# The opening of a fused attention and feed-forward kernel gets another order of instructions on all five engines

## The chip, the cores and the metric

The kernel runs on one core of a Trainium2 chip. The metric is the time of one execution on the device in microseconds (us). The engines of a core are TensorE (PE in the profile; its weight loads are PEld), VectorE (DVE), ScalarE (ACT), GpSimd (POOL) and SyncE (SP), which issues DMAs. Each engine runs its own list of instructions strictly in the order of the list; an instruction that needs the result of another engine waits for a semaphore, and whatever stands behind it on its engine waits too. So the order of each list matters.

## The reference

For 2048 tokens of width 640, the output is the input plus an attention plus a feed-forward layer, both on the normalised input:

```
xn = layernorm(x)
out = x + A(xn, wq, wk, wv, wo) + B(xn, w1, b1, w2, b2)
# A: 32 heads of 20, one K and one V that all heads share
p = softmax((xn@wq per head) @ (xn@wk).T * 20**-0.5);  A = (p @ (xn@wv)) @ wo
# B: hidden width 1536
B = relu(xn@w1 + b1)**2 @ w2 + b2
```

Data are bfloat16.

## The kernel before, in words

**Tiles.** Attention is cut into 32 blocks: 4 groups of 512 queries by 8 groups of 4 heads. In a block the 2048 keys are 16 tiles of 128 (`kt`). The scores of one head and one key tile are one matmul of 128 x 512 into a PSUM bank. A score step `QKj` makes two of them (two heads), and `ACTj` on ScalarE (line 1328) takes both banks at once, writes exp to two slots of `PT`, and so frees the banks. When all four heads of a key tile are there, `PVb_kt` multiplies them with V into PSUM bank 7, where a block's sum grows; this frees the slots. To spare ScalarE, some key tiles go another way (`DQK`, `D1`, `P1` to `P3`, `AD`, `DPV`): VectorE makes a first approximation of exp by arithmetic on bits (`D1`), three shifted copies are made by integer adds on GpSimd or VectorE (`P1` to `P3`, lines 1571 and 1572), and `DPV` multiplies them with V.

**The opening.** The input comes in rows of 128 tokens (`X`, 16 of them). For each row, VectorE takes statistics (`Sa`, `Sb`, `AG`, lines 806 to 808; for rows 2 and 4 ScalarE does, lines 801 and 802), small steps prepare them (`VE`, `NM`), a power gives the reciprocal deviation (`PW` on GpSimd, line 820; for the first four rows `LN` and `EX` on ScalarE), and `XN` writes the normalised row (line 822, on VectorE or GpSimd). TensorE turns it (`T`, lines 866 and 934), VectorE or ScalarE copies that out of PSUM (`TE`), and TensorE makes K (`K`, `KT`), V (`V`) and queries (`Q`, `QC`) from it, which are copied out in turn (`KTe`, `Ve`, `Qe`, `QCe`). `NKr` and `NKs` make the mean of the first keys, which all `KTe` need. The first scores (`QK0`) need the first K and the queries of the first 512 tokens. The first four rows go through first; the other rows are worked in between the first block's scores. Behind them begin the first pieces of the feed-forward layer (`FFN3_f.dt`; `FFN3_f` reads chunk f // 3 of w1, so `FFN3_3` is the first to read chunk `w11`).

**DMA and library.** SyncE issues the loads. `xb` is a copy of the input in DRAM to which GpSimd's `XA` (line 1153) adds the bias by an accumulating DMA of 2.6 MB. `LIB` loads GpSimd's library with the integer add; every pass on GpSimd stands behind it.

**Fills.** Fills are matmuls that TensorE runs while it would wait, to stay busy. A warm-up fill (line 905) writes the bank of the PV sums and is harmless before the first PV step; it may carry a wait on VectorE, taken over from the step it once stood behind. A zero fill (line 901, in the profile under line 729) adds zeros to an open sum; it is harmless only between a block's first and last PV step.

**What sets the order.** A greedy planner first lists all steps with an engine, a duration and what they depend on. Then `PLAN` reorders each engine's list: its tables are strings of small numbers, and each number takes the entry at that place among those that are left (`unpack`; "0*39" takes the first one 39 times). ScalarE has no table, so its list stays as the planner made it. The string "on" chooses for each pass on which engine it runs, and "held" gives each step of GpSimd a step of VectorE that it waits for, or none. `replay` then gives banks and buffers out, and merges the lists; of those, the instructions are made with the waits that are needed.

```
seq[e] = [old[k] for k in unpack(PLAN[e], len(old))]
```

Of the kernel before, what the change touches and what calls it, by code (L numbers as in the profile page):

```python
# [299 lines left out]
def replay(seq, pool, order_all, upool):  # L300
# [32 lines left out]
    while True:  # L333
# [224 lines left out]
def bass_parallel_sum__grouped_kv_mqa__dense_activation_squared_relu__prompt_kernel(nc, A_x, A_wq, A_wk, A_wv, A_wo, B_x, B_w1, B_b1, B_w2, B_b2, out):  # L558
    es = ExitStack()
    with es:  # L560
# [1146 lines left out]
        while True:  # L1707
# [61 lines left out]
            elif unit[0] is not None:  # L1769
# [3 lines left out]
                o = Op(f"{u.name}.{u.k}", "PE", dur, ch())  # L1773
# [368 lines left out]
        fins = replay(seq, pool, order_all, upool)  # L2142
        MODEL["fins"] = fins
        for es_ in ends_of.values():
            es_.sort(key=lambda o: o.start)
            for o in es_:
                o.ends[0], o.ends[1] = o is es_[0], o is es_[-1]
        open_, kept = set(), []
        for o in order_all:
            if o.sums is not None:  # L2150
                (open_.discard if o.ends[1] else open_.add)(0)
            if o.name == "fill" and o.tail and not open_:
                continue
            kept.append(o)
# [99 lines left out]
```

## Time and profile before

| | us |
|---|---|
| median of 3 runs | 665.14 (664.26 to 666.17) |
| the profiled execution | 664.67 |
| its span, first to last instruction | 662.9 |
| first exponential starts | 12.17 |
| TensorE busy | 655.0 (99%) |
| ScalarE busy | 649.2 (98%) |
| VectorE busy | 627.0 (95%) |
| GpSimd busy | 533.1 (80%) |

A row of the timeline gives the start in us, the length in us, the engine, the line of the kernel, the operation, what it writes and reads, its shape and how many like it are merged in the row; a bracket at the end tells how long the engine stood idle before and what ended that. A row of stages gives from and to, the length, the busy time (and the number of instructions) for each engine asked for, the granted TensorE clock, the busy share of the DMA engines and GB/s. Matmuls overlap, so their lengths say less than the distance from one start to the next. `zeros` are zero fills, `hT_tmp,OR` warm-up fills, `qT,kT` scores, `PT,vx` PV steps, `xnT,wk_c` pieces of K, `ident,big` the turning of normalised rows.

### The profile page before, as it was taken

To read this page: it belongs to the slowest core of one execution; us is meant where nothing else is said; L and a number is where in the kernel's file an instruction comes from. 1 tells how busy PE (TensorE), PEld (TensorE's weight loads), DVE (VectorE), ACT (ScalarE), POOL (GpSimd) and SP (SyncE) were. 2 spreads that over 40 slices of the span, in tenths; PEclk is the share of its full clock that TensorE was granted. 3 is DMA by queue.
4 is the path that set the end of the run, shared out by engine and by line. 5 is a ranking of instruction groups with operands and counts; after the bars stand their busy time and mean duration, and the time that the engine had idled before them with its cause. 6 is when DMAs were issued, how large, how long until landed. Compare 5 with 4: busy or idle time off the path is not lost. (4 is left out here: it accounts for less than half of the span.)

```text
span 662.9 us, 22377 instructions
## 1 busy us (share of the span) xinstructions
PE 655.0 (99%) x9569; PEld 212.6 (32%) x9570; DVE 627.0 (95%) x1125; ACT 649.2 (98%) x719; POOL 533.1 (80%) x528
## 2 busy tenths in 40 slices
PE   8999999999999999999999999999999999999997
PEld 4432222332322223333332222333233322223444
DVE  8979999999999999999999999999999999999997
ACT  7999999999999999999999999999999999999995
POOL 1629899898998889898999988888899989799300
PEclk9999999999999999999999999999999999999999
DMA  8694967788997995786956645798798655858731
GB/s 262 188 238 113 189 126 161 163 183 190 191 192 162 184 182 114 135 177 124 184 103 152 126 92 102 153 180 176 150 176 167 130 123 98 171 104 183 136 113 68
DMA packets 53528, 102.09 MB, mean 154 GB/s; under 512 B 15916, under 2 KB 31164, under 8 KB 53364
## 3 DMA queue, kind: packets, MB, share of 16 engines
q0 software_dynamic: 18544, 68.17, 55.7%
q1 hardware_dynamic: 34308, 32.11, 16.7%
q8 instruction: 75, 1.23, 0.8%
q10 hardware_dynamic: 576, 0.38, 0.2%
q14 instruction: 25, 0.20, 0.1%
HBM read 23.26 MB, written 10.01 MB: 50 GB/s over the span
## 5 line engine op out<-in xcount | busy, mean ns | idle before, releaser
L1328 ACT ACTIVATE PT<-ps 128x1024 bf16<-128x1024 f32 x696 | 640.1, 1125 | 1.8 <-PE ps L729 1.4
L1551 DVE TENSOR_SCALAR tx<-ps 128x512 uint16<-128x512 f32 x656 | 423.7, 682 | 20.8 <-PE ps L729 13.5
L1571 POOL INT64_ADD tx<-tx x369 | 391.2, 1130 | 56.7 <-PE ps L729 16.4
L729 PE MATMUL ps<-qT,kT 20*128 20x512 bf16 x2048 | 263.5, 385 | 0.3
L729 PEld LDWEIGHTS ps<-qT,kT 20*128 20x128 bf16 x2048 | 67.8, 91 | 253.1 <-ACT PT L1328 133.5
L729 PE MATMUL ps<-PT,vx 128*32 128x512 bf16 x1392 | 131.4, 384 | 0.0
L729 PE MATMUL ps<-tx,vxs 128*32 128x512 bf16 x1220 | 113.0, 384 | 0.6 <-DMA tx<-tx 0.5
L1588 POOL DMA_DIRECT2D tx<-tx x103 | 102.4, 994 | 7.7 <-POOL tx L1571 6.9
L729 PE MATMUL ps<-w_sb,big 128*32 128x320 bf16 x1536 | 82.7, 302 | 0.0
L729 PE MATMUL ps<-tx,vx 128*32 128x512 bf16 x864 | 81.3, 384 | 0.8 <-DMA tx<-tx 0.7
L729 PE MATMUL ps<-xnT,w_sb 128*32 128x512 bf16 x960 | 79.0, 383 | 0.0
L1572 DVE TENSOR_SCALAR tx<-tx 128x2048 uint16<-128x2048 uint16 x91 | 63.0, 705 | 0.5 <-DMA tx<-tx 0.3
L729 PEld LDWEIGHTS ps<-PT,vx 128*32 128x32 bf16 x1392 | 34.4, 95 | 39.5 <-issue 35.0
L729 PEld LDWEIGHTS ps<-w_sb,big 128*32 128x32 bf16 x1536 | 34.2, 96 | 30.9 <-issue 20.7
L729 PEld LDWEIGHTS ps<-tx,vxs 128*32 128x32 bf16 x1220 | 28.7, 95 | 36.6 <-issue 27.7
L1054 DVE TENSOR_SCALAR hT_tmp<-ps,b1col 128x512 bf16<-128x512 f32 x48 | 35.7, 743 | 1.5 <-PE ps L729 1.3
L729 PE MATMUL ps<-xnT,wq_sb 128*32 128x512 bf16 (+2 forms) x480 | 35.6, 356 | 0.0
L729 PE MATMUL ps<-wo_c,OC 128*32 128x320 bf16 x576 | 31.8, 301 | 0.0
L2117 POOL INT64_ADD tx<-tx x16 | 30.6, 1913 | 0.5
L729 PEld LDWEIGHTS ps<-tx,vx 128*32 128x32 bf16 x864 | 21.0, 95 | 27.1 <-issue 20.5
L729 PEld LDWEIGHTS ps<-xnT,w_sb 128*32 128x32 bf16 x960 | 19.4, 95 | 25.7 <-issue 17.4
L1416 DVE COPY OR<-ps 128x512 f32<-128x512 f32 x30 | 20.4, 681 | 0.9 <-PE ps L729 0.6
(91 smaller groups left out, 242.3 us busy)
## 6 DMA issues: line engine op xcount, KB each, us to landing
tx<-tx POOLq DMA_DIRECT2D x111, 512.0 KB, 5.8
tx<-tx POOLq DMA_DIRECT2D x7, 1024.0 KB, 9.3
w_sb<-in_B_w_dram SPq DMA_DIRECT2D x8, 480.0 KB, 9.3
big<-OR SPq DMA_DIRECT2D x71, 40.0 KB
xb<-in_A_x_dram SPq DMA_DIRECT2D x1, 2560.0 KB, 12.7
xb<-b2r POOLq DMA_DIRECT2D x1, 2560.0 KB, 19.1
xr<-xb SPq DMA_DIRECT2D x16, 160.0 KB, 3.5
out_dram<-out_sb SPq DMA_DIRECT2D x15, 160.0 KB, 3.3
```

The lines of the kernel that those rows point to most:

```text
L729: return lambda e: e.matmul(out_(), l, val(r), start=val(start), stop=val(stop), tile_position=tp, skip_group_check=loose)
L1054: o = Op(f"RL{qc}_{f}", "DVE", 0.66, [lambda e: e.tensor_scalar(out=hT_tmp[:, k % 2, :], in0=ps[:, at(bk), :], scalar1=b1col[:, f:f + 1], ...
L1328: o = Op(f"ACT{st_['j']}", "ACT", ACB + ACM * n, [lambda e: e.activation(out=PT[:, slots[0].n:slots[0].n + n, :], in_=src(), func=AF.Exp, ...
L1416: tn = op(f"TN{b}", "DVE", 0.60, lambda e: e.tensor_copy(out=OR[:, a, :], in_=ps[:, PVB, :]), [lastpv] + or_users[a], prio=0)
L1551: d1 = op(f"D1_{n}_{i}", "DVE", 0.60, lambda e: e.tensor_scalar(out=L()[:, cs].bitcast(U16), in0=ps[:, ref.n, :], scalar1=XA, scalar2=XB, ...
L1571: fns = dict(POOL=lambda e, T=T, j=j: e.int64_add(out=T().bitcast(I64), in0=L().bitcast(I64), in1=TSTEP * j * 0x0001000100010001), DVE=lam ...
L1572: DVE=lambda e, T=T, j=j: e.tensor_scalar(out=T().bitcast(U16), in0=L().bitcast(U16), scalar1=TSTEP * j, scalar2=None, op0=ALU.add))
L1588: p = op(f"AD{a}_{n}", "POOL", ADDUR, lambda e, src=src, dst=dst: e.dma_start(dst(), src(), accum_op=ALU.add), dp + [ad_last.get(k)], dma= ...
L2117: fn = lambda e, x=x: e.int64_add(out=two(*sorted((x["ref"][2].n, x["ref"][3].n))).bitcast(I64), in0=two(*sorted((x["ref"][0].n, x["ref"][ ...
```

## The change

The tables of `PLAN` get other numbers at their beginning, ScalarE gets a table, and the rule that takes fills out is extended. Reading the tables against the planner's list gives this:

- The same steps remain, fills aside. TensorE's first 264 entries differ (of 3205), the 2941 behind are the same in the same order; ScalarE: the first 42 of 719; VectorE: the first 166 of 1125; GpSimd: the first 39; SyncE: the first 33 of 501.
- Pass `P1_0` moves from GpSimd to VectorE, and `P1_4` from VectorE to GpSimd.
- A fill that is not a zero fill is now left out behind the first PV step, and a zero fill is left out ahead of it, as it was when no sum is open. 18 warm-up fills become 16, 11 zero fills in the opening become 7.

TensorE's order to the first scores of the part with the feed-forward layer, w a warm-up fill, F a zero fill, those left out not shown:

```
before
W4 W5 W6 w*15 T0 T1 T2 T3 K0 Q0_0 Q0_1 Q0_3 K1 Q0_2 K2 V0_0 V0_1 K3 QK0 QK1 V0_2 V0_3
w w QK2 w QK4 QK3 T4 T5 PV0_0 F QK5 QK6 KT2.0-2 T6 KT2.3 F KT2.4 QK7 PV0_2 F QK9 QK8 T7
F F PV0_3 PV0_1 F KT3.0 QK11 QK10 KT3.1-4 T8 V1 QK12 T9 F QK13 QK14 PV0_5 KT4.0-4 T10
PV0_4 QK15 T11 QK17 QK16 PV0_6 QK18 KT5.0-4 V2 Q1.0 PV0_7 QK19 QK20 Q1.1-3 T13 T12 QK21
Q1.4 PV0_8 QK22 KT6.0-4 QK23 T14 QK25 QK24 PV0_9 F T15 PV0_11 PV0_10 F QK26 QK27 KT7.0-4
V3 QC0_1.0 QK28 DQK0_2 QC0_1.1-2 QK29 DQK0_0 F QC0_1.3 QK30 DQK0_3 QC0_1.4 PV0_13 F QK31
DQK0_1 PV0_12 QC0_2.0 QK32 B1 PV0_14 QC0_2.1 QK34 QK33 QC0_2.2 PV0_15 FFN3_0.0 QC0_2.3
FFN3_0.1 QC0_2.4 QK35
after
W4 W5 W6 w*11 T0 T1 T2 T3 Q0_1 Q0_0 K0 Q0_3 Q0_2 V0_0 V0_1 K1 V0_2 w QK1 QK0 V0_3 K3 K2
w w QK2 w QK3 QK4 T4 T5 w PV0_0 QK6 QK5 KT2.0-3 T6 KT2.4 F QK7 PV0_1 QK9 QK8 F T7 PV0_3
PV0_2 QK11 QK10 KT3.0-4 V1 T8 QK12 T9 QK13 PV0_4 F QK14 QK15 KT4.0-4 T10 T11 QK16 PV0_6
PV0_5 QK18 QK17 KT5.0-4 V2 PV0_7 QK20 Q1.0-1 QK22 QK19 Q1.2-3 T12 T13 QK21 Q1.4 PV0_8
KT6.0-4 QK23 T14 QK24 QK25 F PV0_10 T15 F PV0_11 QK27 QK26 KT7.0-4 V3 QC0_1.0 QK28 DQK0_2
QC0_1.1 F DQK0_0 QK29 QC0_1.2 PV0_12 DQK0_3 QK30 PV0_9 QC0_1.3-4 QK31 DQK0_1 QC0_2.0 PV0_13
QK32 B1 F PV0_14 QK33 QK34 PV0_15 QC0_2.1-4 FFN3_0.0 QK35
```

ScalarE: ... ACT1 ACT0 ACT2 ACT3 ACT4 ACT6 ACT5 ACT7 to ACT16 ACT18 ACT17 ACT20 ACT22 ACT19 ACT21, in place of ACT0 to ACT22 in order. VectorE, from the first normalised rows on:

```
before
S0a S0b AG0 S1a S1b AG1 S3a S3b AG3 VE2 XN0 XN1 XN2 XN3 TE1 TE3 NKr NKs KTe0_0 S5a KTe0_1 S5b
KTe0_2 KTe0_3 AG5 VE5 S6a Ve0 VE4 S6b AG6 VE6 XN5 XN4 S7b S7a TE4 TE5 AG7 XN6 NM7 VE7 S8a S8b
TE6 KTe2 S9a ...
after
S0a S1b S0b S1a AG0 AG1 S3b S3a VE2 AG3 XN0 XN1 XN2 XN3 TE1 TE3 S5a S5b NKr AG5 NKs VE5 KTe0_0
KTe0_1 S6a S6b XN5 VE4 KTe0_3 KTe0_2 Ve0 S7a XN4 S7b AG6 AG7 VE6 TE4 TE5 S8b XN6 S8a VE7 NM7
AG8 TE6 NM8 KTe2 S9b ...
```

GpSimd and SyncE:

```
GpSimd before: ... PW11 XN11 PW13 PW12 XA PW14 XN14 PW15 XN15 LIB P1_0 P1_1 P3_1 P3_0 P1_2 P2_1 ...
GpSimd after:  ... PW11 XN11 PW12 PW13 PW14 XN14 PW15 XN15 XA LIB P2_1 P1_1 P3_0 P1_2 P2_2 P3_1 ...
SyncE before: X0 X2 wq0 X4 X6 X8 X12 b2 wq xb w11 b1 w10 w23 w20 w12 w13 QD2_0 QD2_1 QD2_2 SM0 w22
              QD2_3 OM0_0 QD3_0 QD3_1 QD3_2 QD4_0 ...
SyncE after:  X0 X2 wq0 X4 X6 X8 b2 X12 wq xb w12 w13 b1 w10 w20 w23 QD2_0 w22 QD2_1 SM0 QD2_2
              QD2_3 QD3_0 QD4_0 QD3_1 QD3_2 w11 OM0_0 ...
```

The diff, cut to its core (the strings are far longer; what follows the opening in them only moves to other lines):

```diff
 PLAN = {
     "PE": (
-        "0*39 1 2 16 21 4 0 28 1*2 2 0 15 1*2 2*3 4 2 21 2*3 30 4 3 2 30 0 1 0 7 0 5 4 0*4 1 0*3 49 0*2 1*7 0*2 1 2 1 0 7 1*7 0*3 1*3 3 2*2 1 0 1*7 2 3 2 0 2 3 2 0*2 1*11 2 5 2*2 "
+        "0*6 41 3 1 87 0 82 0 46 6 3 0*2 47 4*4 43 6 5 4*2 5 6*2 4 8 3 6 5*2 11 4 3 0 3*2 4 37 3 6 4*2 1 26 2 4 3 4*4 5 4 2 3 0 1 4 3 11 2 0 1 0 6 5 0*10 1 47 0 7 1*6 2*2 1 0 8 0 "
...
+    "ACT": (
+        "0*19 1 0*4 1 0*11 1 0 1 2"),
...
     "on": (
-        "01000000000000100000100110000000010000100000001001000100001000000000000000001010000100000000110011100001000010000200001000010001100001010000001100011000010010100011010010"
+        "11000000000000100000000110000000010000100000001001000100001000000000000000001010000100000000110011100001000010000200001000010001100001010000001100011000010010100011010010"
...
-        open_, kept = set(), []
+        open_, kept, begun = set(), [], False
         for o in order_all:
             if o.sums is not None:
                 (open_.discard if o.ends[1] else open_.add)(0)
-            if o.name == "fill" and o.tail and not open_:
+                begun = True
+            if o.name == "fill" and (not open_ if o.tail else begun):
                 continue
             kept.append(o)
```

152 rows, old and new, of the table PLAN are left out of this document.

## The prediction

> **What bounds the kernel now.** I read the page first, then the exponentials of ScalarE by stage, then the timeline of the opening engine by engine, then the DMA issues. Part 1 of the page says that TensorE and ScalarE are both nearly always busy:
>
> ```profile
> PE 655.0 (99%) x9569; PEld 212.6 (32%) x9570; DVE 627.0 (95%) x1125; ACT 649.2 (98%) x719; POOL 533.1 (80%) x528
> ```
>
> The second view takes line 1328 alone (the 696 exponentials of ScalarE) over four stages: length, busy time, count.
>
> ```profile
> 12.17:44.97 32.80, 32.63 (x35) 1.00 0.84 214
> 44.97:150.00 105.03, 105.03 (x116) 1.00 0.75 164
> 150.00:350.00 200.00, 199.44 (x218) 1.00 0.81 162
> 350.00:653.85 303.85, 303.03 (x330) 1.00 0.68 138
> ```
>
> 105.03 / 116 is 0.905 us for an exponential: that is the floor, ScalarE never without a tile. The opening took 32.80 / 35 = 0.937. So 35 x (0.937 - 0.905) = 1.1 us is all that a better order of the opening can give back on ScalarE, unless the first exponential starts earlier. That bounds the gain at 0.17% before anything is said of the change.
>
> Next, who made ScalarE late. Of TensorE I show the steps that stand just ahead of a late exponential, and some that give the price of a step:
>
> ```profile
> 11.35 0.46 PE L729 MATMUL ps<-xnT,wk_c 128*20 128x128 bf16 x20
> 11.74 0.40 PE L729 MATMUL ps<-qT,kT 20*128 20x512 bf16 x4
> 20.05 0.60 PE L729 MATMUL ps<-PT,vx 128*32 128x512 bf16 x8
> 20.48 0.39 PE L729 MATMUL ps<-kT,zeros 128*32 128x512 bf16 x4
> 20.69 0.28 PE L729 MATMUL ps<-xnT,wk_c 128*20 128x256 bf16 x4
> 32.09 0.39 PE L729 MATMUL ps<-qT,kT 20*128 20x512 bf16 x2
> 32.61 0.72 PE L729 MATMUL ps<-xnT,wk_c 128*20 128x256 bf16 x20
> 33.27 0.39 PE L729 MATMUL ps<-qT,kT 20*128 20x512 bf16 x2
> 44.39 0.39 PE L729 MATMUL ps<-qT,kT 20*128 20x512 bf16 x3
> 12.17 8.36 ACT L1328 ACTIVATE PT<-ps 128x1024 bf16<-128x1024 f32 x9 [0.23 <-PE ps L729]
> 33.70 1.02 ACT L1328 ACTIVATE PT<-ps 128x1024 bf16<-128x1024 f32 x1
> ```
>
> The score step QK0 with QK1 starts at 11.74 and its exponential at 12.17; QK23 starts at 33.27 and its exponential at 33.70. So an exponential starts 0.43 us after its score step, or one floor (0.905) after the exponential before it, whichever is later. QK23 was the late side.
>
> The same rows price the steps of TensorE: two PV steps fill 20.05 to 20.48, 0.215 each; a fill 20.48 to 20.69, 0.21; five K pieces and a change of tiling 32.61 to 33.27, 0.66, so 0.11 a piece and 0.11 a change; a score step with the change to and from it about 0.43. With these I added up all steps from QK0 (11.74) to QK35 (44.39): 30.60 us against 32.65 on the chip. The other 2.05 us are stalls, most of them early:
>
> ```profile
> 13.11 0.10 PEld L905 LDWEIGHTS ps<-hT_tmp,OR 128*128 128x128 bf16 x1 [0.70 <-DVE mv L811]
> 14.71 0.69 PEld L934 LDWEIGHTS ps<-ident,big 128*128 128x128 bf16 x10 [0.46 <-DVE big L822]
> 16.03 0.10 PEld L729 LDWEIGHTS ps<-qT,kT 20*128 20x128 bf16 x2 [0.42 <-ACT PT L1328]
> ```
>
> Here a warm-up fill waits for VectorE's statistics, then the transposes T4 and T5 for the normalised rows XN4 and XN5, then QK5 for a PSUM bank. 0.20 more goes at 32.09 to 32.61 (a score step needs 0.32, the pieces of KT6 started 0.52 later: they waited for TE12), and some at T13, T15 and QK18.
>
> **The change, part by part.** Nothing is computed differently.
>
> *Fills.* Behind the first score step, 11 zero fills become 7, and 3 warm-up fills become 4 (one more stands just ahead of it):
>
> ```profile
> 12.17:44.97 32.80, 4.14 (x44) 1.00 0.84 214
> L905 PE MATMUL ps<-hT_tmp,OR x17: 379/389/632, 2.6 to 13.8; 128*128 128x512 bf16 x17
> ```
>
> (44 matmuls with zeros are 11 fills of four.) That is -4 x 0.21 = -0.84 and +0.21 us. K2 and K3 now come behind the first scores and V0_2 ahead of them, +0.56 - 0.13 (a K step is 20 matmuls, 11.35 to 11.74 with the change of tiling). The score steps stand in 25 bunches in both orders. Added up to QK57, beyond which both orders hold the same steps, the old one is 50.49 us of work and the new one 50.37. So the new order has only 0.1 us less to do; the rest must come from stalls.
>
> *Ahead of the first exponential.* The rows of VectorE:
>
> ```profile
> 9.05 0.49 DVE L869 COPY xnT<-ps 128x640 bf16<-128x640 bf16 x1 [0.17 <-PE ps L866]
> 9.46 0.28 DVE L883 TENSOR_REDUCE nk<-ps 128x1 f32<-128x128 f32 x1
> 9.78 0.15 DVE L884 TENSOR_SCALAR nk<-nk 128x1 f32<-128x1 f32 x1
> 9.97 0.35 DVE L885 TENSOR_SCALAR kT<-ps,nk 128x128 bf16<-128x128 f32 x1
> 10.23 0.49 DVE L806 BATCH_NORM_STATS2 OR<-tx 128x6 f32<-128x320 bf16 x1
> 10.63 0.34 DVE L885 TENSOR_SCALAR kT<-ps,nk 128x128 bf16<-128x128 f32 x1
> ```
>
> S5a and S5b move ahead of NKr, at 0.40 each (10.23 to 10.63), so KTe0_0 goes from 9.97 to about 10.8, ending 11.15. TensorE no longer needs K2 and K3 before QK1. Its row of work from Q0_1 at 9.06 (TE1 ends at 8.88) is five steps of 0.28, the V pair 0.45 with its changes, K1 0.39, V0_2 0.13, a fill 0.32: QK1 at 11.75, against 11.74. Without the fill it would be 11.43, so the fill is not free; what it covers is nothing that I can see. First exponential: unchanged, 12.18.
>
> *The early stalls.* The fill behind QK1 now waits for S1b and AG5, long done. XN5 moves ahead of S6b's followers and is ready near 13.0, XN4 near 14.65 as before (it needs VE4, which needs ScalarE), so T4 still waits until about 14.7; QK6 and QK5 start at 16.0 instead of 16.03 and 16.30. K2 and K3 fill time in which TensorE stood. Gain at this place 0.25 us.
>
> *From 16 to 45 us.* I walked the new orders of TensorE, VectorE and GpSimd with the prices above (0.40 a statistic, and as much a TE or KTe of the later blocks), each step behind the one before it on its engine and behind what it reads. Starts that come out, estimates all: QK8/QK9 18.6 (was 18.87); QK10 20.6 (20.91), held by the banks of the eighth exponential; KT4 24.5 (24.29); QK16 26.1 (26.41); KT5 27.3 (27.50); QK22 29.8, where the new order puts it ahead of QK21; KT6 32.2 (32.61), held by TE13; QK23 32.8 (33.27); QK26 35.4 (36.18); QK35 43.7 (44.39). One exponential is still late, the one behind QK23, by about 0.3 us; PV0_1 goes ahead of QK8, so that the tenth exponential finds its buffer free. The exponential of QK35 then starts 12.2 + 35 x 0.905 + 0.35 = 44.2 against 44.97: 0.75 us gained on ScalarE. TensorE gains less. At QK35 it has 0.7, but one step of the feed-forward (0.22) is put off behind QK35, and by QK57 it is 0.1 us of work and 0.3 of stalls ahead, 0.4 in all. Behind the opening both are close to their limits, so I take 0.5.
>
> *GpSimd.* XA moves behind the last normalised row, and with it the library load that follows it:
>
> ```profile
> 28.53 1.81 POOL L1153 DMA_DIRECT2D xb<-b2r  x1
> 34.02 0.87 POOL L822 TENSOR_SCALAR big<-tx,mv,rstd 128x640 bf16<-128x640 bf16 x1
> 46.98 1.04 POOL L1571 INT64_ADD tx<-tx  x1 [12.09 <-PE ps L729]
> 48.65 3.07 POOL L1571 INT64_ADD tx<-tx  x3 [0.63 <-DVE tx L1551]
> ```
>
> XN15 would end near 34.0 (34.89), XA 1.8 us later, the load takes 12.1 (34.89 to 46.98): first pass at 48.0. The first pass needed there, P1_0, goes to VectorE (P1_4 comes the other way), and P2_1 and P1_1, next in line, began at 48.65 before. P3_0 ends at 51.1, DPV1_11_3 wants it near 52.2; P3_1 ends about 55.2 and DPV1_15_3 wants it then. Cost between 0 and 0.5 us, taken as 0.
>
> *SyncE.* The load w11 goes from 18 us to behind QD3_2, about 49.2 us. Two landing rows, of the w1 loads and of XA, an old wait of SyncE, and the first step that reads w11 (FFN3_3.0):
>
> ```profile
> DMA to landing us min/median/max: 6.5/10.7/15.8
> DMA to landing us min/median/max: 19.1/19.1/19.1
> 37.01 7.73 SPq L766 DMA_DIRECT2D w_sb<-in_B_w_dram  x2
> 60.23 0.61 PE L729 MATMUL ps<-xnT,w_sb 128*32 128x512 bf16 x8
> ```
>
> w11 lands between 49.2 + 6.5 = 55.7 and 49.2 + 15.8 = 65.0. The long landings are those of loads that ran beside XA; XA now runs from about 34.1 to 53.2, so only a third of w11's flight lies beside it: about 56, ahead of 59.7. Taken as 0, upper end 5.3 us.
>
> *The sum.* 664.67 us (span 662.9 and 1.8 around it) - 0.5 = 664.2 for a run like the profiled one; that one lies 0.5 under the median shown, so 664.6 for the median. What a measurement tells from no change is 0.3%, 2.0 us: the forecast is no change that can be told.
>
> **Rivals.** *w11 late (slower).* If w11 lands at L beyond 59.7, FFN3_3.0 and all of TensorE behind it wait L - 59.7; past 62.3 the kernel is slower by over 0.3%. For it: SyncE itself hung 7 us on such a load (37.01). Against: those stood four deep. At the upper end 664.6 + 5.3 = 669.9; middle 667.5.
>
> *TensorE cold.* TensorE starts slow and speeds up between 4.28 and 4.61:
>
> ```profile
> 1.31 1.46 PE L861 MATMUL ps<-hT_tmp,OR 128*128 128x512 bf16 x3 [1.31 <-DVE PT L738]
> 4.28 0.15 PEld L905 LDWEIGHTS ps<-hT_tmp,OR 128*128 128x128 bf16 x1 [0.28 <-issue]
> 4.61 0.10 PEld L905 LDWEIGHTS ps<-hT_tmp,OR 128*128 128x128 bf16 x1 [0.19 <-issue]
> 7.47 1.54 PE L866 MATMUL ps<-ident,big 128*128 128x128 bf16 x20
> ```
>
> (0.15 us a weight load, then 0.10; in the row of line 905, matmuls of 632 ns, then 379.) The first ten matmuls stay as they are and end near 5.2. In the new order the next fill waits for S3b, near 6.3: a pause of 1.1 us, where the longest later pause of the old timeline is about 0.7 (the row at 13.11). If that slows the clock again for the 3.1 us that it took to speed up (1.31 to about 4.4), the 4.3 us from T0 (7.47) to QK0 grow by about 1.6: 666.2. Nothing in this trace shows such a fall. The Trainium skill, TensorE: Matmul & The Clock Gate, section Part 1: The HAM clock gate, says that the clock halves after an idle window of about 3.4 us; by that rule 1.1 us is too short and the time stays 664.6. No run here shows it yet.
>
> *Gain lost behind the opening.* From 150 us on an exponential takes 200 / 218 = 0.917 us, so something else than ScalarE holds there. If those waits sit on transfers that do not move, 0.5 us is eaten and the time is 665.1.
>
> *More than the opening.* The bound of 1.1 us and a lucky fit behind the seam: 663.0 at best, just past the limit.
>
> **Numbers.** Forecast 0.55; gain lost 0.17; cold 0.08, these three within 0.3%; w11 late 0.12, of which 0.10 past the limit; other stalls of a wrong order 0.03, slower; more than the opening 0.05 (0.04 in the faster class). Same 0.83, slower 0.13, faster 0.04. The range 663.3 to 666.7 holds the forecast, the lost gain, the cold clock and runs 0.2% apart; the late load's upper half is left out.
>
> **What would show it.** 35 exponentials from the first one on in about 32.0 us instead of 32.80; the first near 12.2; zero fills 28 matmuls; first GpSimd pass near 48.0; FFN3_3.0 near 59.7 without a wait for a DMA; the stretch 45 to 150 still 0.905 an exponential. Wrong would be: matmuls of 500 ns and more after 5 us, a gap ahead of FFN3_3.0, DPV1_15_3 waiting for GpSimd, or a first exponential past 12.5.

## The result, and the profile after

The changed kernel takes 666.15 us (median; 665.08 to 669.66) against 664.85 us of the kernel before (663.98 to 668.31) in the same comparison. The ratio is 1.0021, with a 95% interval from 1.0012 to 1.0029: slower by 0.2%. That is inside the 0.3% in which the forecast called it no change and inside the range, but the forecast said 0.5 us faster and it is 1.3 us slower. The profiled execution took 665.46 us with a span of 663.7 us.

Part 1 of the page of the changed kernel gives the engines as before:

```profile
PE 655.1 (99%) x9550; PEld 211.3 (32%) x9552; DVE 626.4 (94%) x1125; ACT 649.3 (98%) x719; POOL 533.5 (80%) x529
```

Nothing is to be seen in such shares. The view by stages shows it: of the exponentials alone (line 1330 in this kernel) the length of a stage, the busy time and the count. First the changed kernel from its first exponential to the 36th, from there to the 58th or 59th, and on; then the kernel before over the same second stage.

```profile
11.80:44.62 32.82, 32.20 (x35) 1.00 0.74 208
44.62:65.60 20.98, 20.40 (x24) 1.00 0.74 167
65.60:150.00 84.40, 84.39 (x93) 1.00 0.78 163
150.00:350.00 200.00, 199.48 (x218) 1.00 0.81 162
350.00:654.58 304.58, 303.75 (x331) 1.00 0.68 138
```

```profile
44.97:65.02 20.05, 20.05 (x23) 1.00 0.62 165
```

The opening takes 32.82 us where it took 32.80: the forecast 32.0 did not come. The second stage, in which the forecast changed nothing, takes 20.98 instead of 20.05 us. (The exponential that starts at the edge is counted in one kernel and not in the other; the lengths are between the same exponentials.) In each of the two stages ScalarE stands still once. The timeline of ScalarE in the changed kernel, where exponentials that follow each other without a gap are one row:

```profile
11.80 17.52 ACT L1330 ACTIVATE PT<-ps 128x1024 bf16<-128x1024 f32 x19 [0.41 <-PE ps L731]
29.87 26.86 ACT L1330 ACTIVATE PT<-ps 128x1024 bf16<-128x1024 f32 x29 [0.55 <-PE ps L731]
57.31 5.60 ACT L1330 ACTIVATE PT<-ps 128x1024 bf16<-128x1024 f32 x6 [0.58 <-PE ps L731]
```

The exponentials before 29.87 come every 0.9035 us; the one at 29.87 comes 1.79 us after the one before it, so 0.89 late, and the one at 57.31 (number 48, counted from 0 as in ACT48) 0.87 late. (Exponentials that follow each other overlap by some 0.3 us, so the idle time in the bracket is less than the lateness.) What TensorE did there:

```profile
25.80 0.39 PE L731 MATMUL ps<-qT,kT 20*128 20x512 bf16 x2 [0.15 <-ACT PT L1330]
26.12 0.61 PE L731 MATMUL ps<-PT,vx 128*32 128x512 bf16 x8
26.71 0.39 PE L731 MATMUL ps<-qT,kT 20*128 20x512 bf16 x2
27.54 0.39 PE L731 MATMUL ps<-qT,kT 20*128 20x512 bf16 x2 [0.44 <-ACT PT L1330]
27.86 0.73 PE L731 MATMUL ps<-xnT,wk_c 128*20 128x256 bf16 x20
...
55.80 0.39 PE L731 MATMUL ps<-qT,kT 20*128 20x512 bf16 x2 [0.46 <-DMA qT<-QCr]
```

*The first stall.* The rows at 26.71 and 27.54 are QK18 and QK17. They stand side by side in the list, and two score steps side by side start together (the row of QK22 and QK19 in this kernel is one row of four matmuls). But one of the two banks that QK17 got is freed by the exponential of QK16 (27.49 us), so the pair is split: 0.44 us of idle time, and another 0.32 until the next step can start. KT5 starts at 27.86. From there TensorE has no gap up to 55 us; it keeps the lag.

*The second stall.* The step at 55.80 is DQK4_0 with DQK4_1. Their queries come by the four DMAs QD2, whose last packet lands at 55.66 us by the updates of their semaphore (54.20 in the kernel before, where DQK4_1 reads them at 55.35). They were issued between 41.4 and 46.1 us and stand in SyncE's queue behind the load w23 (lands at 49.4) and, three of them, behind w22 (55.3), while XA runs from 34.4 to 54.7 us.

The other things that the prediction named: the fills, the first pass of GpSimd behind XA, and the pause of TensorE ahead of T0, each from its own view of the changed kernel (the line's group; the timelines of GpSimd and TensorE).

```profile
L731 PE MATMUL ps<-kT,zeros x28: 379/389/390, 17.2 to 41.8; 128*32 128x512 bf16 x28
```

```profile
34.38 1.80 POOL L1155 DMA_DIRECT2D xb<-b2r  x1
48.70 3.07 POOL L1573 INT64_ADD tx<-tx  x3 [12.52 <-DVE vxs L923]
```

```profile
6.26 1.04 PE L907 MATMUL ps<-hT_tmp,OR 128*128 128x512 bf16 x4 [0.84 <-DVE OR L809]
```

### The profile page after: what moved, and what is told of

Read it like the earlier page. It is cut to its first block, busy times and chain, and to the rows that moved or that the text cites. A ratio compares the mean times of both kernels' runs of the same rounds, so it can differ in the third digit from the quotient of the medians.

```text
span 663.7 us, 22341 instructions
## 1 busy us (share of the span) xinstructions
PE 655.1 (99%) x9550; PEld 211.3 (32%) x9552; DVE 626.4 (94%) x1125; ACT 649.3 (98%) x719; POOL 533.5 (80%) x529
## 4 chain that ended last, share of the span: by engine, by line
PE 87%; DMA 5%; DVE 4%; ACT 2%; POOL 0%; issue 0%; SPq 0%; DVEq 0%; POOLq 0%
PE ps L731 87%; DMA tx<-tx 3%; ACT PT L1330 2%; DVE tx L1553 2%; DMA qT<-QCr 2%; DVE tx L1574 1%; POOL tx L1573 0%; PE ps L936 0%; PE ps L868 0%; PE ps L966 0%; DVE OR L809 0%; PE ps L907 0%; DVE ident L745 0%; DVE PT L1666 0%; DVE OR L808 0%
## 5 line engine op out<-in xcount | busy, mean ns | idle before, releaser
L1330 ACT ACTIVATE PT<-ps 128x1024 bf16<-128x1024 f32 x696 | 640.2, 1125 | 3.0 <-PE ps L731 2.6
L1573 POOL INT64_ADD tx<-tx x371 | 393.8, 1134 | 55.3 <-DVE vxs L923 12.5
```

The costliest lines, as they stand in the source:

```text
L1330: o = Op(f"ACT{st_['j']}", "ACT", ACB + ACM * n, [lambda e: e.activation(out=PT[:, slots[0].n:slots[0].n + n, :], in_=src(), func=AF.Exp, ...
L1573: fns = dict(POOL=lambda e, T=T, j=j: e.int64_add(out=T().bitcast(I64), in0=L().bitcast(I64), in1=TSTEP * j * 0x0001000100010001), DVE=lam ...
```

## The experiments

Each kernel is the changed one or the one before with a few steps moved. The moves are made once the tables have been applied, ahead of the giving out of banks:

```diff
+        for e, name, ahead in (("POOL", "XA", "PW13"), ("SP", "w10", "w12")):
+            live = {o.name: o for o in seq[e] if o.on}
+            seq[e].remove(live[name])
+            seq[e].insert(seq[e].index(live[ahead]), live[name])
```

Below stand only the moves (engine, step, the step that it goes ahead of). All results side by side; "opening" is from the first exponential to the 36th, "next" from there to the 58th, QD2 the landing of the last packet of these queries, the ratio that to the kernel before in the same comparison, with its interval. All but median and ratio are read from one profiled execution; those of e3 (670.68 us) and e10 (669.91 us) are the slowest of their kernels.

| | opening | next | QD2 | median | ratio |
|---|---|---|---|---|---|
| before | 32.80 | 20.05 | 54.20 | 664.85 | |
| changed | 32.82 | 20.98 | 55.66 | 666.15 | 1.0021 (1.0012 to 1.0029) |
| e1 XA early | 32.96 | 20.24 | 50.64 | 665.47 | 1.0013 (1.0001 to 1.0025) |
| e2 KT5 first | 33.41 | 20.77 | 56.05 | 666.24 | 1.0026 (1.0015 to 1.0037) |
| e3 DQK4 later | 32.96 | 21.57 | 56.51 | 667.18 | 1.0038 (1.0025 to 1.0051) |
| e4 old, XA late | 32.29 | 31.90 | 59.57 | 676.85 | 1.0169 (1.0138 to 1.0199) |
| e5 w22 late | 33.38 | 20.23 | 53.92 | 664.79 | 1.0003 (0.9994 to 1.0012) |
| e6 w22 late, KT5 | 32.22 | 20.23 | 52.79 | 664.32 | 0.9990 (0.998 to 1.000) |
| e7 old, XA early | 32.91 | 20.75 | 51.94 | 665.63 | 1.0017 (1.0008 to 1.0025) |
| e8 old, XA late, loads | 32.31 | 20.35 | 51.14 | 664.32 | 0.9996 (0.9987 to 1.0005) |
| e9 old, XA late, w12 | 32.29 | 24.68 | 57.86 | 669.00 | 1.0101 (1.0026 to 1.0176) |
| e10 old, XA late, w12, w13 | 34.12 | 23.88 | 58.88 | 667.05 | 1.0034 (1.0018 to 1.0049) |
| e11 longer pause | 32.83 | 21.48 | 57.60 | 668.56 | 1.0054 (1.0038 to 1.0069) |

In e1, e2, e3 and e5 the third exponential came 0.15, 0.55, 0.14 and 0.56 us late, which stands in "opening". They have the instructions of the changed kernel up to there, whose profiled execution has no such wait: it differs from execution to execution, and without it their openings are 32.81, 32.86, 32.82 and 32.82.

**e1: XA early.** Moves on the changed kernel, with XA's wait for a step of VectorE taken away:

```diff
+ ("POOL", "XA", "PW13"), ("SP", "w10", "w12")
```

> The changed kernel with two moves: XA (the accumulating DMA of 2.6 MB) goes ahead of PW13 on GpSimd, about 26.6 us instead of 34.4 us, without its wait for a step of VectorE, and the load w10 goes ahead of w12 on SyncE so that it does not fall beside XA. Theory: the second stall of ScalarE (exponential 48 starts at 57.31 us, 0.86 us late) comes from the query DMAs QD2, whose last packet lands at 55.66 us because they stand behind XA in the DMA engines until 54.7 us. Then QD2 lands before 52 us here, the score step DQK4_0 starts near 55.3 us instead of 55.80, exponential 48 at 56.45, the last exponential of that stage (57) 0.86 us earlier, and the time is 0.9 us under that of the changed kernel (ratio to the kernel before about 1.001 instead of 1.0021). Rival: DQK4_0 waits for the PSUM bank that VectorE frees (D1_3_2); then exponential 48 stays at 57.3 us and the time stays. The first stall (exponential 20, 29.87 us) stays by both.

QD2 landed at 50.64 us, and no wait of TensorE is left there; exponential 48 is 0.13 late instead of 0.87. The median came 0.7 us under the changed kernel; the intervals of the two ratios overlap, so it is the trace that decides. The theory of the DMA stands; the bank of VectorE as the cause falls.

**e2: KT5 first.**

```diff
+ ("PE", "QK17", "V2.0"), ("PE", "QK20", "V2.0"), ("PE", "QK22", "PV0_7")
```

> The changed kernel with three score steps moved on TensorE: QK17 and QK20 go behind KT5 (QK17 waited for the bank of exponential 16, and KT5, which needs no bank of ScalarE, stood behind it), and QK22 ahead of PV0_7. Theory: the first stall of ScalarE (the exponential of QK20 starts at 29.87 us, 0.88 us late) is that wait of QK17 in front of KT5. Then KT5 starts near 27.1 us instead of 27.86, the exponential of QK20 at 28.98, that of QK35 at 43.8 instead of 44.62, and the time is 0.85 us under that of the changed kernel (ratio about 1.001). Rival: what is late is VectorE's copy KTe5 or XN12 and not KT5; then at least 0.5 us of the stall stays at the same exponential, and the time moves by less than 0.4 us. The second stall (exponential 48) stays 0.86 us long by both or gets longer, since it ends with a DMA at a fixed time: if it is a DMA, exponential 48 stays at 57.3 us and the total does not move at all; that would mean that the two stalls do not add up.

The exponential of QK20 came in time, but those of QK21 and QK23 came 0.58 and 0.52 late, and the opening stayed at 32.86. KT5 did start 0.8 us earlier against the third exponential. But this order takes QK22 away from QK19, leaves QK17 alone too, and puts QK20 where it waits 0.28 us for KTe5: one more bunch of 0.32 and that wait are what had been won. The second stall became shorter (0.66), since it ends with a transfer. So an earlier KT5 alone gains nothing; the bunches count.

**e3: DQK4 later.**

```diff
+ ("PE", "DQK4_0", "DQK4_2"), ("PE", "DQK4_1", "DQK4_2")
```

> The changed kernel with DQK4_0 and DQK4_1 put behind QK48 on TensorE, the DMAs left as they are. Theory (queries of QD2 land at 55.66 us): the PV steps and QK48 no longer stand behind the late queries, QK48 starts near 55.95 us, exponential 48 at 56.45 instead of 57.31, and VectorE's next D1 at about 56.7 instead of 56.2. Time 0.5 to 0.9 us under that of the changed kernel, ratio 1.001. Rival (the bank of D1_3_2): QK48 now takes that bank, free since 54.7 us by the records, and starts early too, so exponential 48 gains likewise; this run tells whether the stall is only an order of TensorE, not what it waits for.

Exponential 48 came in time and no step waits for the queries any more, but the next two exponentials came 0.76 and 0.61 late, and the time is 1.0 us over the changed kernel instead of 0.5 to 0.9 under it. Timeline of TensorE in this kernel:

```profile
56.56 0.60 PE L731 MATMUL ps<-qT,kT 20*128 20x512 bf16 x5
57.31 0.62 PE L731 MATMUL ps<-xnT,w_sb 128*32 128x512 bf16 x8
58.23 0.39 PE L731 MATMUL ps<-qT,kT 20*128 20x512 bf16 x3 [0.30 <-ACT PT L1330]
...
59.09 0.38 PE L731 MATMUL ps<-qT,kT 20*128 20x512 bf16 x1
59.73 0.39 PE L731 MATMUL ps<-qT,kT 20*128 20x512 bf16 x2 [0.26 <-ACT PT L1330]
```

With the order the banks were given out anew: QK49 and QK50 now take those of the exponentials just ahead of theirs (48 and 49; in the changed kernel 47 and 48), and QK50 is split from DQK4_3. Neither theory had expected that. The run says that the wait was for the queries, and that moving their readers brings other waits.

**e4: the kernel before with XA late, and nothing else.**

```diff
+ ("POOL", "XA", "LIB")
```

> The kernel before with one part of the change alone: XA behind XN15 on GpSimd, ahead of the library load. Theory: SyncE's loads w23, w20, w12 and w13 and the queries QD2 (last packet 54.2 us in the kernel before) are held as long as XA's bytes are in the queues, so QD2 lands about 5.8 us later, near 60, and DQK4_1 (55.35 us) waits for it: a stall of 4 to 5 us of TensorE and ScalarE between 55 and 60 us, time 668 to 670 us, ratio 1.005 to 1.008. Rival (VectorE's bank): nothing of the sort; the first pass of GpSimd comes about 1 us later, and the time moves by less than 0.5 us.

The stall came as expected, and then something more. Timeline of TensorE, and its windows (length, busy time, count, granted clock), in this kernel:

```profile
59.71 0.62 PE L729 MATMUL ps<-qT,kT 20*128 20x512 bf16 x4 [4.48 <-DMA qT<-QCr]
```

```profile
55.28:58.69 3.41, 0.00 (x0) 1.00 0.99 289
58.69:82.58 23.89, 22.87 (x169) 0.50 0.41 75
82.58:86.00 3.42, 3.42 (x47) 1.00 0.81 153
```

TensorE stood 4.48 us for the queries, and for 24 us afterwards it was granted half its clock; that makes 12 us out of a stall of 4.5. And one thing is better than in the kernel before: the opening takes 32.29 us. The timelines of VectorE in the kernel before, and in e8, which has XA late as well:

```profile
29.02 1.46 DVE L822 TENSOR_SCALAR big<-tx,mv,rstd 128x640 bf16<-128x640 bf16 x2
```

```profile
29.05 0.80 DVE L822 TENSOR_SCALAR big<-tx,mv,rstd 128x640 bf16<-128x640 bf16 x2
```

These are XN12 and XN13. While GpSimd issued XA, from 28.53 to 30.34 us, they took 0.86 and 0.68 us; without XA beside them, 0.44 each, and what follows on VectorE comes 0.65 earlier. The late exponentials at 31.7, 33.7 and 36.6 us of the kernel before are gone with it.

**e5: w22 late**, on the changed kernel:

```diff
+ ("SP", "w22", "OM0_0")
```

> The changed kernel with one load moved: w22 (480 KB) goes behind w11 on SyncE, so that the queries QD2_1 to QD2_3 no longer stand behind it in the queue; XA stays late. Theory (a queue is worked off in order, and XA only makes the load ahead of the queries slow): QD2's last packet lands near 50 us instead of 55.66, DQK4_0 no longer waits, exponential 48 starts 0.87 us earlier against exponential 47, and the time is 0.8 us under that of the changed kernel (ratio to the kernel before 1.001). Rival (all transfers of the core wait until XA is through, whatever stands ahead of them): QD2 lands near 55 us again and the stall stays.

One load moved, and the second stall is gone (20.23). The time is 1.4 us under the changed kernel by the medians, 1.2 by the ratios. QD2 landed at 53.92 us, though, not near 50. Their semaphore shows how. It is raised ten times for each of the four DMAs: in the changed kernel ten times by 49.64 us, behind w23, and the other thirty only from 54.19 on, behind w22; here ten times by 50.35 and the others from 50.83 to 53.92, while XA ran to 54.20. So the queries were not held until XA was through, as the rival said, and not as fast as the theory said: XA makes loads and queries slow (w23 took 13.5 us beside it in the changed kernel, the load just ahead 3.6), and what stands behind a load of 480 KB as well is later by 1.7 us more (55.66 against 53.92).

**e6: w22 late, and the pair mended.**

```diff
+ ("SP", "w22", "OM0_0"), ("PE", "QK17", "V2.0"), ("PE", "QK20", "PV0_7")
```

> The changed kernel with w22 behind w11 as in the run with that move alone, and QK17 behind KT5, QK20 ahead of PV0_7 on TensorE; QK22 stays beside QK19, so that one score step less stands alone than in the run that moved three. Theory (the first stall is a pair of score steps split by the wait for the bank of exponential 16: 0.44 us idle and 0.33 for a second bunch): the 35 exponentials of the opening take 32.3 us instead of 32.82, the second stall is gone, time 1.3 us under that of the changed kernel, ratio 1.000. Rival (TensorE has so much to do from 26 to 36 us that a stall only moves): the 35 exponentials take 32.7 to 32.9 us and the ratio is that of the run with w22 alone.

The 35 exponentials took 32.22 us. Timeline of TensorE in this kernel:

```profile
26.82 0.39 PE L731 MATMUL ps<-qT,kT 20*128 20x512 bf16 x2
27.14 0.73 PE L731 MATMUL ps<-xnT,wk_c 128*20 128x256 bf16 x20
27.80 0.39 PE L731 MATMUL ps<-qT,kT 20*128 20x512 bf16 x2
28.12 0.66 PE L966 MATMUL ps<-wv_c,xnT 128*128 128x20 bf16 x20
28.71 0.39 PE L731 MATMUL ps<-qT,kT 20*128 20x512 bf16 x2
29.03 0.40 PE L731 MATMUL ps<-PT,vx 128*32 128x512 bf16 x4
29.25 0.60 PE L731 MATMUL ps<-xnT,wq_sb 128*20 128x512 bf16 x8
29.79 0.40 PE L731 MATMUL ps<-qT,kT 20*128 20x512 bf16 x4
```

No gap, and QK22 and QK19 stay one row of four matmuls. It is 1.8 us under the changed kernel and 0.4 under the kernel before, with an interval that ends at 1.000. With e5 it also says what the two stalls cost by the medians: 1.4 us for the queries, 0.5 for the split pair. The second figure is not firm, as the intervals of e5 and e6 overlap; in the opening of the profiles the pair costs 0.60 (32.82 against 32.22).

**e7: the kernel before with XA early.**

```diff
+ ("POOL", "XA", "PW13")
```

> The kernel before with one move: XA ahead of PW13 on GpSimd, about 25.9 us instead of 28.53. In the kernel before, VectorE's XN13 ran 1.05 us beside XA's issue, and with XA late only 0.43 us. Theory (the issue of XA on GpSimd slows that operation of VectorE, and the late rows T13 and KT6 with it): XN13 takes 0.43 us here too, the 35 exponentials of the opening take 32.3 us instead of 32.80, QD2 lands by 52 us, time 0.5 us under the kernel before (ratio 0.9992). Rival: the opening got shorter in the run with XA late because XN14 and XN15 no longer stood behind XA's 1.8 us; here they still stand clear of it as PW13 comes at 27.7 us, so this rival too expects a gain, but with XN13 at 1.05 us beside whatever GpSimd then runs.

XN12 and XN13 took 0.44 us each (the 1.05 us of the expectation was a misreading of the row of both) and the exponentials up to 42 us came in time, as expected. Then two came 0.6 us late each, and the time is 0.9 us over the kernel before, not 0.5 under it. Timeline of TensorE:

```profile
42.15 0.39 PE L729 MATMUL ps<-qT,kT 20*128 20x512 bf16 x2
42.83 0.39 PE L729 MATMUL ps<-qT,kT 20*128 20x512 bf16 x2 [0.29 <-ACT PT L1328]
...
46.17 0.39 PE L729 MATMUL ps<-qT,kT 20*128 20x512 bf16 x2 [0.35 <-ACT PT L1328]
```

QK34 and QK33, one row in the kernel before, are split: with XA elsewhere `replay` gave QK33 the banks of the exponential of QK32 instead of those of QK31; the row at 46.17 is QK36, with a bank of the exponential of QK35 instead of that of QK34. The order of TensorE was the same in both. That is the first stall of the changed kernel again, twice, and made by the banks alone.

**e8: the kernel before with XA late and the loads out of its way.** The SyncE order is not quite that of the change: w11 stays early, and w22 goes behind all of QD2, where the change has it ahead of three of the four.

```diff
+ ("POOL", "XA", "LIB"), ("SP", "w12", "w23"), ("SP", "w13", "w23"), ("SP", "w20", "w23"), ("SP", "w22", "OM0_0")
```

> The kernel before with XA behind XN15, as in the run that lost 12 us, but with the loads out of its way: w12, w13 and w20 go ahead of w23 on SyncE (where each waits only for its buffer) and w22 behind QD2_3. So this is the GpSimd and SyncE half of the change with the old order of TensorE, ScalarE and VectorE. Theory: w12 and w13 land near 32 us before XA starts, QD2 lands by 51 us, the 4.5 us stall of TensorE is gone, its clock stays at full speed, and the opening keeps its 0.5 us: time 0.5 us under the kernel before (ratio 0.9992). Rival (XA late costs in itself, by the library load or the first pass of GpSimd 1 us later): the time is 0.3 us or more over the kernel before.

The opening took 32.31 us, QD2 landed at 51.14, the 4.5 us are gone. The median is 0.4 under the kernel before, but the interval holds 1. XA late does not cost in itself; it costs where loads that are needed early stand beside it. The median is also that of e6: no run shows that the new orders of TensorE, ScalarE and VectorE give anything beyond what moving XA and the loads gives.

**e9 and e10: fewer loads ahead of the queries.** On the kernel of e4, w12, then w12 and w13, go ahead of w23:

```diff
+ ("POOL", "XA", "LIB"), ("SP", "w12", "w23")
+ ("POOL", "XA", "LIB"), ("SP", "w12", "w23"), ("SP", "w13", "w23")
```

> The run that lost 12 us (the kernel before with XA behind XN15) with one of the four loads taken out of the way: w12 goes ahead of w23, so three loads of 480 KB instead of four stand ahead of the queries QD2 while XA runs. Theory (the queue is worked off in order, and a load takes 1.7 us of it, the distance of their landings there): QD2's last packet lands near 57.9 us instead of 59.57, TensorE stands for 2.8 us instead of 4.48. Whether its clock then falls is open: the pause of 0.84 us in the changed kernel did nothing, that of 4.48 us halved the clock. By a gate between 2.8 and 4.48 us the time is 667 us; by a gate below 2.8 us the clock is 0.50 again for some 20 us and the time is 672 us or more. By the Trainium skill, TensorE: Matmul & The Clock Gate, section Part 1: The HAM clock gate, an idle window of about 3.4 us is needed, so 667 us.

QD2 landed at 57.86 us and TensorE stood for 2.77 us, both as worked out from 1.7 us a load. But the clock fell. Windows of TensorE in e9:

```profile
55.29:58.70 3.41, 0.71 (x12) 1.00 0.60 171
58.70:62.11 3.41, 3.41 (x34) 0.50 0.09 22
```

The time was 669.0 us (ratio 1.0101, 1.0026 to 1.0176), between the two that were named.

> The same with w12 and w13 ahead of w23, two loads instead of four. Theory: QD2 lands near 56.2 us, TensorE stands for 1.1 us, its clock stays at 1.00, time 665.5 us (the kernel before, less 0.5 us of the opening, plus the stall). Rival (the hold does not depend on the bytes ahead of the queries but on the end of XA alone): QD2 lands right after XA as in the run with four loads, within 1 us of 59.6 us.

667.05 us (1.0034, 1.0018 to 1.0049). In the profiled execution, the slowest of ten, the opening was 1.8 us late (a wait at 13 us, below), so QD2's 58.88 us and XA's end at 56.8 compare with 57.1 and 55.0: the second load gained 0.8 us, not 1.7. TensorE stood for 1.97 us. So the rule of 1.7 us a load does not go on. The count of loads left one out: QD2_3 stands behind w22 too, which landed at 58.67 us here. How much of the hold is XA's own end is not settled. Three of the ten executions kept a mean granted clock of 1.000 and took 665.55 to 666.12 us, near the 665.5 of the theory; the six at 0.995 to 0.997 took 666.97 to 669.91. So more than half of what this kernel lost was the clock.

**e11: a longer pause ahead of T0**, the changed kernel without four warm-up fills:

```diff
+        seq["PE"] = [o for o in seq["PE"] if o not in [x for x in seq["PE"] if x.name == "fill" and not x.tail][7:11]]
```

> The changed kernel without the four warm-up fills between 6.26 us and the first turned row T0: TensorE stands from 5.42 to about 7.2 us, 1.8 us instead of 0.84. Theory (a pause of this size leaves the clock): the turning T0 to T3 and the steps up to QK0 take the 4.2 us that they took, the first exponential starts at 11.8 to 12.2 us, and the time is that of the changed kernel. Rival (a cold TensorE): matmuls of 500 ns and more behind the pause, the first exponential 1.5 us later, time 1.5 us over the changed kernel.

The rival was right in kind: the first exponential came at 13.23 us and the time was 668.56 us (1.0054, 1.0038 to 1.0069), 2.4 us over the changed kernel where it said 1.5. In the profile 0.5 us of that lies at the second stall (exponential 48 is 1.38 late instead of 0.87). Timeline and windows of TensorE in e11:

```profile
7.21 1.55 PE L868 MATMUL ps<-ident,big 128*128 128x128 bf16 x20 [1.61 <-DVE big L824]
```

```profile
5.32:8.73 3.41, 1.80 (x26) 1.00 1.01 333
8.73:12.14 3.41, 3.41 (x127) 0.50 0.83 264
12.14:15.55 3.41, 3.41 (x81) 1.00 1.37 542
```

## Why the prediction was wrong, and where it was right

**The gain in the opening: wrong.** The failed step is the walk "From 16 to 45 us", at "KT5 27.3". Counted from the first scores (forecast 11.75, measured 11.37), TensorE is within 0.25 us of the walk up to QK16 (14.35 forecast, 14.43 measured) and 0.94 behind it at KT5 (15.55 and 16.49); most of that lag stays to QK35 (31.95 and 32.67). Between QK16 and KT5 lie two PV steps, which took what they were priced at, and the pair QK18 and QK17. The walk took the pair as one bunch. It did not ask which bank each half gets, and one of QK17's was free 0.8 us later. This one wait made the exponential 0.89 late, more than the 0.75 us that the walk had gained. e6 has the pair mended and takes 32.22 us, close to the 32.0 of the forecast.

**The old stalls: half wrong.** Part of what the old order lost (exponentials at 31.7, 33.7 and 36.6 us) was put down to order; e4, e7 and e8 show that it was XN12 and XN13, stretched by XA. Moving XA was priced on GpSimd's own list and never as a neighbour of VectorE. It is worth 0.5 us of the opening.

**SyncE: wrong, and this gives the sign.** The step "w11 lands ... Taken as 0" was right for w11: it landed at 57.1 us (forecast 56), and FFN3_3.0 ran at 60.91 without a wait. But it followed only the load that the table moves far. The queries QD2 also run while XA runs in its new place; they are needed at 55 us and had 1.15 us to spare before. They were not in the sum at all: 0.87 us on ScalarE in the profile, and with them out of the way the kernel is as fast as the kernel before (e5, 1.4 us less by the medians).

**The first exponential: near, by luck.** Forecast 12.18. In six profiled executions with the new beginning it came at 11.80, 11.81, 11.80, 11.90, 11.93 and 12.18 us, but in four of them the third exponential gave 0.14 to 0.56 back, so that with it they stand at 11.80 to 12.36. What made the third late is open: in e5 the second matmul of QK2 starts 0.66 us after the first, and the profile shows nothing that it waits for.

**GpSimd: right, by another wait.** First pass at 48.70 us (forecast 48.0), held by VectorE's `vxs`, which ended at 48.58, and not by the library. The 12.1 us that were read as the library's load were too long: in e4 the first pass came 9.9 us behind XA's issue (45.90 and 35.97). The later passes fit the forecast; DPV1_15_3 ran at 56.56 us and P3_1 had ended at 55.23. **Fills: right**, 28 zero matmuls.

**TensorE cold: right for this kernel, for a wrong reason.** The pause was 0.84 us (forecast 1.1) and the clock stayed. But the rule that was leaned on would have let 1.6 us pass as well, and e11 shows that it does not.

**Gain lost behind the opening: could not happen to the changed kernel**, which had no gain. e6 shows such a loss in its profiled execution (665.26 us, the slowest of eleven): 0.67 us ahead of the kernel before at the 117th exponential (118.53 against 119.20 us), 0.13 behind at the 201st (196.81 against 196.68). Of that, 0.13 lies at 164 us, where TensorE waits for one of GpSimd's adding DMAs, 0.51 us against 0.38, and 0.56 at one exponential at 172 us, which was not followed up. It does not stay lost: at the 501st exponential e6 is 0.59 ahead again, at the last 0.09 behind.

## What to carry to other kernels

When an order is changed, ask of each pair of steps that should run side by side which buffer each half gets and what frees it: a split pair costs its wait and its second slot, and a tuned order can lose its whole gain to one. When a large transfer is moved, list everything else that is in flight in its new place, with the time at which it is needed and its slack, and look also at what runs on the engine next door while it is issued. Price a stall on TensorE at more than its length once it fills a good part of a window of the clock.

## What the runs showed of the hardware

**The clock gate looks at fixed windows, and a window need not be idle.** Within an execution the granted clock changes only at distances that are multiples of 3.41 us (in e10 at 16.13, 19.54, 60.50 and 63.92 us), and where this grid lies differs from one execution to the next. A window of the grid with TensorE busy for 0.71 us (e9), 1.80 us (e11), 2.13 us (e10) or 2.21 us (e3) of 3.41 was followed by one at half clock; one with 2.25 us (e5) or 2.57 us (the changed kernel, with the pause of 0.84 us) was not. The windows of e10, of e3, of e5 and of the changed kernel (for the last two the grid is counted back from the fall of the clock at their end, at 663.08 and 663.71 us):

```profile
12.72:16.13 3.41, 2.13 (x18) 1.00 1.22 474
16.13:19.54 3.41, 3.41 (x40) 0.50 1.01 403
```

```profile
164.26:167.68 3.42, 2.21 (x39) 1.00 0.97 201
167.68:174.50 6.82, 6.82 (x74) 0.50 0.89 181
```

```profile
4.31:7.72 3.41, 2.25 (x16) 1.00 0.97 299
```

```profile
4.94:8.35 3.41, 2.57 (x22) 1.00 1.02 340
```

By busy time the limit here lies near 2.2 us; it can't be placed closer, as the ends of matmuls are modelled. A wait of 1.22 us was enough (e10, at 13 us, where a fill waited for VectorE's statistics), and one of 1.16 us (e5, ahead of the fill at 6.27 us) was not. Whether the busy time of a window counts or the longest wait in it, these rows do not tell: both sort them alike. The Trainium skill, TensorE: Matmul & The Clock Gate, section Part 1: The HAM clock gate, gives free-running windows of about 3.4 us, which agrees, and says that the clock halves after at least one idle window, which does not agree with these rows; the measurement decides. The four warm-up fills ahead of T0 hold the clock, as e11 shows.

**A wholly idle window costs far more.** After a window with nothing in it (e4) the half clock lasted 23.89 us, seven windows, though TensorE was busy for 22.87 of them; after the part-filled ones of e9, e10 and e11 it lasted one, after that of e3 two. The seven windows were seen in one profile; what ended them is not shown.

**An accumulating DMA slows its neighbours twice.** While GpSimd issued it (1.80 us), two operations of VectorE from SBUF to SBUF (XN12 and XN13, in the one profile that has them there) took 0.86 and 0.68 us instead of 0.44. Not every operation of VectorE is slowed: in e1 and e7 its statistics and its copies out of PSUM ran beside the issue in 0.47 to 0.48 us, their usual length. And while its 2.6 MB ran (20 us), loads of SyncE were slow: in the changed kernel w23 took 13.5 us (35.91 to 49.38; 8.8 in e8), the 480 KB just ahead of it 3.6 (32.20 to 35.77). What stands in SyncE's queue behind such a load waits with it: the queries of 20 KB that were issued from 42.9 us on landed between 54.2 and 55.7 behind w22. With XA just as late but w22 behind them, they landed between 46.3 and 51.1 us, ahead of XA's end at 53.3 (e8), so they do not wait for XA itself to end. The Trainium skill, DMA: Bandwidth & Descriptors, section Queues, rings and completion order, says that a DMA's semaphore is raised only after every earlier write of the same DMA engine, across its queues. No run here tells that rule from the shared rate of the engines.
